# Attention with a cached K and V on one core: K transposed as 64-row tiles into two PSUM banks, P transposed into score banks, loads of 256 KB paced by TensorE operations

## The chip, the cores and the metric

The kernel runs on one core of a Trainium2 chip. The metric is the device time of one execution in microseconds (us). A time below is either the median of unprofiled runs, or comes from one profiled execution, whose trace gives the start and length of every instruction. The engines are TensorE (PE in the profile; PEld is its weight load), VectorE (DVE), ScalarE (ACT), GpSimd (POOL) and SyncE (SP), which issues the loads.

## The reference

Two blocks, A and B, do the same thing with their own data; their outputs are joined on the last axis. All data are bf16. For one block:

```python
B, Sq, D, H, Sk, Dh = 16, 64, 640, 32, 512, 128
q = (x @ wq).reshape(B, Sq, H, Dh).transpose(0, 2, 1, 3)
scores = einsum("bhqd,bhkd->bhqk", q, k_cache) * Dh ** -0.5
p = softmax(scores, axis=-1)
o = einsum("bhqk,bhkd->bhqd", p, v_cache)
out = o.transpose(0, 2, 1, 3).reshape(B, Sq, H * Dh) @ wo
```

K and V of one block are 67 MB each, so 268 MB of cache are read for the two, and with the weights (21 MB) and x about 292 MB. The scores contract over Dh, which is the last axis of K in memory: K has to be transposed on the chip before the score matmul can use it, and P has to be transposed before it meets V.

## The kernel before, in words

**Steps, macros, chunks, groups, passes.** A step is one head of a pair of batches; its 2 x 64 query rows fill 128 partitions. A macro (index m) is two heads, a chunk is two macros (four heads), a group is 16 heads of one pair of batches (four chunks), and a pass is the eight pairs of batches with one half of the heads of one block. There are 4 passes, 32 groups, 128 chunks, 256 macros and 512 steps. One chunk reads 1.05 MB of K and as much of V.

**The work of a macro.** On TensorE: KX transposes K (L451-459), eight 128x128 transposes for each of the two batches (j = 0, 1) into PSUM bank 7; QP2 makes q of two heads (L469, ten matmuls); SM makes the scores of one step (L487, one matmul of 512 columns for each batch, side by side in the two 64-column halves of the array); TR2 transposes P (L528, eight 128x128 transposes into bank 6); PV2 multiplies by V (L549, sixteen matmuls of 64 columns); OP2 multiplies by the first 512 columns of wo (L569, two matmuls). OX does the last 128 columns of wo for a whole group at once (L580, sixteen matmuls), and for the very last group in two parts. The other engines move the results on: KE copies transposed K out of PSUM (DVE, L462, 1024 columns each); QE2 copies q and OE2 copies o (ACT, L482 and L564, 256 columns each); MX takes the row maximum (DVE, L502); EX is the exponential with the row sum (ACT, L508); RC2 the reciprocal (DVE); NM scales P (POOL, L520); TE2 or TA2 copies transposed P out, on DVE (L539) or on ACT (L544). OVP and OXP keep the sum of the first half of the heads in SBUF, OVF and OXF add the second half, ST stores it.

**K by DMA.** In the 11 groups named in TGROUPS (by_dma, L98) the K of the second batch is not transposed by TensorE: one DMA_TRANSPOSE for the whole group (LDKT, L647) writes it to kd_sb, and KX and KE of j = 1 are left out.

**PSUM.** Bank 0 holds the output sum, bank 1 q and o (half each), banks 2 to 5 the scores of four steps in turn, bank 6 transposed P, bank 7 transposed K.

**Order.** Each engine runs a fixed list. The templates PE_T, ACT_T, DVE_T and POOL_T in Cfg (L29-43) give the order of one chunk: a kind, an offset in macros, and a planned time within PERIOD (6.7 us). build_plan (L69) unrolls them. With the offset, KX runs two to four macros ahead of SM of the same macro, PV2 two or three behind it, OP2 three or four behind it. Who waits for whom follows from named resources (the banks, the ring slots, the loaded tiles), and prune_waits (L321) drops waits that others imply. TensorE takes its list strictly in order.

**Loads.** All loads go out from SP, in the order of their planned first use, each as soon as its ring slot is free by the plan (L252-264): K and V in pieces of 512 KB into a K ring of 4 chunks (NKB) and a V ring of 5 (NVB), wq and wo in pieces of 640 KB (four heads) into 6 slots each, x by DMA_TRANSPOSE (LDX, L641). A load waits only for TensorE operations that still read its slot. SP issues in order, so a load that waits holds all later ones.

The lines that the profile names: L457 KX, L466 KE, L475 QP2, L484 QE2, L496 SM, L505 MX, L511 EX, L517 RC2, L525 NM, L534 TR2, L541 TE2, L546 TA2, L558 PV2, L566 OE2, L574 OP2, L584 OX, L602 OVF, L607 OXF, L630 LDWQ, L638 LDWO, L644 LDX, L651 LDKT, L660 LDV, L664 LDK. The functions that the change touches, and what calls them:

Of the kernel before, what the change touches and what calls it, by code (L numbers as in the profile page):

```python
# [14 lines left out]
class Cfg:  # L15
    G = 4
    HH = 16
    NKB = 4
    NW = 6
    TGROUPS = (4, 6, 11, 13, 15, 19, 21, 23, 27, 29, 31)  # L20
    TLEAD = 1.0
    NVB = 5
    XLEAD = 1.5
    NQ = 3
    NKT = 5
    NP = 4
    NPN = 4
    NT = 2
    NO = 9  # L29
    NR = 8  # L30
    NS = 4
    PERIOD = 6.7
    PE_T = (("SM", 0, 0, 0.0), ("SM", 0, 1, 0.21), ("SM", 1, 0, 0.43), ("SM", 1, 1, 0.64), ("KX", 2, 1, 0.98),
            ("PV2", -3, 0, 1.43), ("TR2", -2, 0, 1.9), ("OP2", -4, 0, 2.35), ("KX", 3, 1, 2.78), ("QP2", 3, 0, 3.23),
            ("OP2", -3, 0, 3.79), ("OX", -3, 0, 4.2), ("KX", 3, 0, 4.22), ("PV2", -2, 0, 4.67), ("TR2", -1, 0, 5.14),
            ("KX", 4, 0, 5.59), ("QP2", 4, 0, 6.04))
    ACT_T = (("EX", 0, 0, 1.13), ("OE2", -3, 0, 2.1), ("EX", 0, 1, 2.49), ("TA2", -2, 0, 3.15), ("QE2", 3, 0, 4.0),
             ("EX", 1, 0, 4.4), ("OXP", -3, 0, 5.2), ("OE2", -2, 0, 5.34), ("EX", 1, 1, 5.73), ("OVP", -3, 0, 6.4),
             ("QE2", 4, 0, 6.65), ("ST", -3, 0, 6.68))
    DVE_T = (("MX", 0, 0, 0.44), ("MX", 0, 1, 1.06), ("RC2", -1, 0, 1.66), ("KE", 2, 1, 1.68), ("MX", 1, 0, 2.3),  # L40
             ("TE2", -2, 0, 2.6), ("RC2", 0, 0, 3.3), ("KE", 3, 1, 3.43), ("MX", 1, 1, 4.1), ("KE", 3, 0, 4.87),
             ("OXF", -3, 0, 5.3), ("OVF", -3, 0, 5.5), ("TE2", -1, 0, 5.79), ("KE", 4, 0, 6.4))
    POOL_T = (("NM", -1, 0, 1.95), ("NM", -1, 1, 2.8), ("NM", 0, 0, 4.2), ("NM", 0, 1, 5.05))
    TAIL_SPLIT = 2
    SLOT_NS = 3400.0
    DMA_NS = dict(LDK=3100.0, LDKT=9600.0, LDV=3100.0, LDWQ=3900.0, LDWO=4300.0, LDX=700.0)


class Op:
# [3 lines left out]
    def __init__(self, eng, kind, idx, reads=(), writes=(), dur=0.0, ts=None, aux=None):  # L53
        self.eng = eng
        self.kind = kind
        self.idx = idx
        self.reads = tuple(reads)
        self.writes = tuple(writes)
        self.sem = None
        self.count = None  # L60
        self.deps = []
        self.waits = []
        self.dur = dur
        self.ts = ts
        self.aux = aux
        self.dma = kind in ("LDK", "LDKT", "LDV", "LDX", "LDWQ", "LDWO", "ST")


def build_plan(dims, cfg):  # L69
# [3 lines left out]
    assert H % HH == 0 and HH % G == 0 and G % 2 == 0 and cfg.NR % 2 == 0 and B % 2 == 0  # L73
# [11 lines left out]
    MPP = NBP * MPG  # L85
    MPC = G // 2
# [11 lines left out]
    def by_dma(m, j=1):  # L98
        return j == 1 and m // MPG in cfg.TGROUPS

    tstart = [m for m in range(0, NMAC, MPG) if by_dma(m)]

# [3 lines left out]
    def kslot(m, j):  # L106
        return (4 * (m // 2) + (j if m % 2 == 0 else 3 - j)) % cfg.NKT

    def on_act(m):
        return m % 2 == 0 and not by_dma(min(m + 4, NMAC - 1))  # L110

    def make_op(kind, m, sub, ts):
        g0, g1 = 2 * m, 2 * m + 1
        if kind in ("KX", "KE") and by_dma(m, sub):
            return None
        ps_, bp, grp, h0 = step_info(g0)
        c = g0 // G
        if kind == "KX":
            return mk("pe", "KX", (m, sub), [("kn", c % cfg.NKB, g0 % G), ("kn", c % cfg.NKB, g1 % G), ("ident",)],
                      [("KTB",)], ts)  # L120
        if kind == "KE":
            return mk("dve", "KE", (m, sub), [], [("KTB",), ("ktp", kslot(m, sub))], ts)
        if kind in ("MX", "EX", "NM"):
            g = 2 * m + sub
            r = g % cfg.NR
            if kind == "MX":
                return mk("dve", "MX", g, [], [("SB", g % cfg.NS), ("negmax", r)], ts)
            if kind == "EX":
                return mk("act", "EX", g, [("negmax", r)], [("SB", g % cfg.NS), ("p", g % cfg.NP), ("rowsum", r)], ts)
            return mk("pool", "NM", g, [("p", g % cfg.NP), ("recip", r)], [("pn", g % cfg.NPN)], ts)  # L130
        r0, r1 = g0 % cfg.NR, g1 % cfg.NR
        if kind == "QP2":
            return mk("pe", "QP2", m, [("xT", bp), ("wq", wslot(ps_, h0 // G))], [("QOB",)], ts)
        if kind == "QE2":
            return mk("act", "QE2", m, [], [("QOB",), ("qT", m % cfg.NQ)], ts)
        if kind == "SM":
            kt = [("ktp", kslot(m, 0)), ("kd",) if by_dma(m) else ("ktp", kslot(m, 1))]
            return mk("pe", "SM", (m, sub), [("qT", m % cfg.NQ)] + kt, [("SB", (2 * m + sub) % cfg.NS)], ts)
        if kind == "RC2":
            return mk("dve", "RC2", m, [("rowsum", r0), ("rowsum", r1)], [("recip", r0), ("recip", r1)], ts)  # L140
        if kind == "TR2":
            return mk("pe", "TR2", m, [("pn", g0 % cfg.NPN), ("pn", g1 % cfg.NPN), ("ident",)], [("PTB",)], ts)
        if kind in ("TE2", "TA2"):
            if (kind == "TA2") != on_act(m):
                return None
            return mk("dve" if kind == "TE2" else "act", kind, m, [], [("PTB",), ("pT", m % cfg.NT)], ts)
        if kind == "PV2":
            return mk("pe", "PV2", m, [("pT", m % cfg.NT), ("v", c % cfg.NVB, g0 % G), ("v", c % cfg.NVB, g1 % G)],
                      [("QOB",)], ts)
        if kind == "OE2":  # L150
            return mk("act", "OE2", m, [], [("QOB",), ("oT", m % cfg.NO)], ts)
        if kind == "OP2":
            return mk("pe", "OP2", m, [("oT", m % cfg.NO), ("wo", wslot(ps_, h0 // G))], [("OUTB",)], ts)
        lo = grp * MPG
        last = h0 + 2 == SPB
        if kind == "OX":
            hi = m + 1
            if grp == NGRP - 1 and h0 + 6 == SPB:
                pass
            elif not last:  # L160
                return None
            elif grp == NGRP - 1:
                lo = m - 1
            return mk("pe", "OX", m, [("oT", i % cfg.NO) for i in range(lo, hi)]
                      + [("wo", wslot(ps_, i)) for i in sorted({(2 * i % SPB) // G for i in range(lo, hi)})],
                      [("SB", 0)], ts, aux=(lo, hi))
        if not last:
            return None
        if kind in ("OVP", "OXP") and ps_ % NHALF == 0:
            return mk("act", kind, m, [], [("OUTB",) if kind == "OVP" else ("SB", 0), ("outp", bp, kind[1])], ts,  # L170
                      aux=grp)
        if kind in ("OVF", "OXF") and ps_ % NHALF == 1:
            return mk("dve", kind, m, [("outp", bp, kind[1])],
                      [("OUTB",) if kind == "OVF" else ("SB", 0), ("out_sb", kind[1])], ts, aux=grp)
        if kind == "ST" and ps_ % NHALF == 1:
            return mk("act", "ST", m, [("out_sb", "V"), ("out_sb", "X")], [("out_dram", grp)], ts, aux=grp)
        return None

    templates = {"pe": cfg.PE_T, "dve": cfg.DVE_T, "pool": cfg.POOL_T, "act": cfg.ACT_T}
    at = {}  # L180
    for eng, tmpl in templates.items():
        offs = [t[1] for t in tmpl]
        for k in range(-(max(offs) + 1) // 2 - 1, (NMAC - min(offs)) // 2 + 1):
            for kind, off, sub, t in tmpl:
                m = 2 * k + off
                if 0 <= m < NMAC:
                    op = make_op(kind, m, sub, 2 * k + 2 * t / cfg.PERIOD)
                    if op is not None:
                        progs[eng].append(op)
                        at[kind, m, sub] = op.ts  # L190
# [10 lines left out]
    for ps_ in range(NPASS):  # L201
        for j in range(HG):
            m0 = ps_ * MPP + j * MPC
            i = ps_ * HG + j
            rq = ro = NEG
            if i >= cfg.NW:
                end = ((i - cfg.NW) // HG + 1) * MPP
                rq = at["QP2", end - MPG + ((i - cfg.NW) % HG) * MPC + MPC - 1, 0]
                ro = at["OX", end - 1, 0]
            add(rq, at["QP2", m0, 0], at["QP2", m0, 0], 0, "LDWQ", (ps_, j), [("wq", wslot(ps_, j))], (ps_, j),  # L210
                cfg.DMA_NS["LDWQ"] * G / 8.0)
            add(ro, at["OP2", m0, 0], at["OP2", m0, 0], 3, "LDWO", (ps_, j), [("wo", wslot(ps_, j))], (ps_, j),
                cfg.DMA_NS["LDWO"] * G / 8.0)

    def tload(m):
        return at["SM", m, 0] - cfg.TLEAD

# [540 lines left out]
```

## Time and profile before

| what | value |
|---|---|
| median of 3 runs | 898.71 us (897.31 to 901.26) |
| the profiled execution's own time | 900.23 us |
| its span, first to last instruction | 898.5 us |
| instructions | 33204 |
| mean granted TensorE clock | 0.996 |
| loaded and stored by DMA | 296.81 MB, mean 330 GB/s |
| issues of K and V | 211 of K and 254 of V with 512 KB, 2 and 4 with 256 KB |
| K by DMA_TRANSPOSE | 11 issues, median 17.9 us to landing |

Busy times are summed lengths of instructions. A matmul's length in the trace is its latency, and neighbours overlap, so what a block of matmuls costs is read from the distance between the start of its first and the start of the next block's first. The same holds for VectorE and ScalarE, where the end of one instruction overlaps the start of the next.

### The profile page before, as it was taken

How to read it: one execution, taken by the hardware profiler on the slowest of the kernel's cores; microseconds unless marked ns; L12 is line 12 of the kernel's file. 1: busy time of each engine (PE TensorE's matmuls, PEld its weight loads, DVE VectorE, ACT ScalarE, POOL GpSimd, SP SyncE). 2: the span in 40 equal slices, each digit the busy share in tenths (PEclk: the TensorE clock that was granted, in tenths of full speed). 3: DMA queues.
4: the chain of work that ended last, by engine and by line, in shares of the span. 5: the costliest groups of instructions: out<-in, count | busy, mean ns of one | idle time of the engine just before them, and what ended most of it. 6: DMA issues, size and time to landing. Idle time of an engine off the chain costs nothing.

```text
span 898.5 us, 33204 instructions
## 1 busy us (share of the span) xinstructions
PE 857.5 (95%) x14016; PEld 691.1 (77%) x14144; DVE 746.6 (83%) x1398; ACT 628.0 (70%) x1651; POOL 413.8 (46%) x518
## 2 busy tenths in 40 slices
PE   4999989999999999999998998999999999999997
PEld 3777777878888877878786787778778777787875
DVE  2888878888888888888887887888888798888896
ACT  1776766777777777767676776777777676776774
POOL 0544444445444454544444444445454444545453
PEclk9999999999999999999999999999999999999999
DMA  9999999999999999999999999999999999999992
GB/s 304 336 340 365 318 272 365 295 361 365 363 366 368 286 361 322 319 369 270 364 361 368 367 260 365 309 324 366 294 363 363 367 370 284 367 286 365 315 333 77
DMA packets 315172, 296.81 MB, mean 330 GB/s; under 512 B 109200, under 2 KB 260752, under 8 KB 315024
## 3 DMA queue, kind: packets, MB, share of 16 engines
q1 hardware_dynamic: 312720, 292.06, 106.3%
q10 hardware_dynamic: 2304, 2.62, 0.9%
q8 instruction: 111, 1.82, 0.9%
q14 instruction: 37, 0.30, 0.1%
HBM read 266.34 MB, written 2.62 MB: 299 GB/s over the span
## 4 chain that ended last, share of the span: by engine, by line
PE 78%; DMA 9%; SPq 7%; DVE 3%; issue 1%; ACT 1%; DVEq 0%; ACTq 0%
PE ps L457 20%; PE ps L475 14%; PE ps L496 12%; PE ps L558 11%; PE ps L534 10%; PE ps L574 9%; DMA kn_ring<-in_B_k_cache_dram 5%; DMA kn_ring<-in_A_k_cache_dram 4%; SPq L651 3%; PE ps L584 3%; SPq L644 2%; DVE ktp_ring L466 1%; SPq L664 1%; DMA wq_sb<-in_A_wq_dram 1%; DVE negmax L505 1%
## 5 line engine op out<-in xcount | busy, mean ns | idle before, releaser
L525 POOL TENSOR_SCALAR pn_ring<-p_ring,recip 128x512 bf16<-128x512 bf16 x512 | 413.1, 843 | 476.1 <-DVE recip L517 475.7
L511 ACT ACTIVATE p_ring<-ps,negmax 128x512 bf16<-128x512 f32 x512 | 350.1, 684 | 100.0 <-DVE negmax L505 100.0
L466 DVE COPY ktp_ring<-ps 128x1024 bf16<-128x1024 bf16 x424 | 290.0, 684 | 82.1 <-PE ps L457 67.2
L505 DVE TENSOR_REDUCE negmax<-ps 128x1 f32<-128x512 f32 x512 | 337.3, 680 | 15.2 <-PE ps L496 4.9
L457 PEld LDWEIGHTS ps<-ident,kn_ring 128*128 128x128 bf16 x3392 | 205.3, 98 | 108.5 <-issue 46.5
L457 PE MATMUL ps<-ident,kn_ring 128*128 128x128 bf16 x3392 | 263.6, 221 | 21.1 <-DMA kn_ring<-in_A_k_cache_dram 11.8
L475 PE MATMUL ps<-xT_sb,wq_sb 128*128 128x128 bf16 x2560 | 187.8, 221 | 1.3 <-DMA wq_sb<-in_A_wq_dram 0.6
L558 PE MATMUL ps<-pT_ring,v_ring 128*128 128x64 bf16 x4096 | 162.0, 193 | 8.6 <-DMA v_ring<-in_B_v_cache_dram 3.1
L475 PEld LDWEIGHTS ps<-xT_sb,wq_sb 128*128 128x128 bf16 x2560 | 154.4, 99 | 16.9 <-ACT oT_ring L566 15.8
L558 PEld LDWEIGHTS ps<-pT_ring,v_ring 128*128 128x128 bf16 x4096 | 141.9, 98 | 28.5 <-issue 26.5
L484 ACT ACTIVATE qT_ring<-ps 128x256 bf16<-128x256 f32 x256 | 98.3, 384 | 86.1 <-PE ps L475 86.0
L534 PE MATMUL ps<-ident,pn_ring 128*128 128x128 bf16 x2048 | 156.4, 219 | 0.0
L566 ACT ACTIVATE oT_ring<-ps 128x256 bf16<-128x256 f32 x256 | 97.6, 381 | 75.3 <-PE ps L558 68.1
L541 DVE COPY pT_ring<-ps 128x1024 bf16<-128x1024 bf16 x174 | 119.5, 687 | 35.5 <-PE ps L534 35.5
L496 PE MATMUL ps<-ktp_ring,qT_ring 128*64 128x512 bf16 x848 | 137.3, 391 | 0.0
L574 PE MATMUL ps<-wo_sb,oT_ring 128*128 128x512 bf16 x384 | 124.5, 379 | 6.8
L534 PEld LDWEIGHTS ps<-ident,pn_ring 128*128 128x128 bf16 x2048 | 118.5, 98 | 0.0
L511 ACT ACTIVATION_READ_ACCUMULATOR p_ring<-ps,negmax 128x1 f32 x512 | 103.1, 201 | 0.0
L546 ACT ACTIVATE pT_ring<-ps 128x1024 bf16<-128x1024 bf16 x82 | 84.0, 1024 | 0.0
L496 PEld LDWEIGHTS ps<-ktp_ring,qT_ring 128*64 128x64 bf16 x848 | 47.1, 110 | 41.0 <-issue 2.1
L517 DVE RECIPROCAL recip<-rowsum 128x2 f32<-128x2 f32 x256 | 40.9, 160 | 14.7 <-ACT p_ring L511 14.6
L496 PE MATMUL ps<-kd_sb,qT_ring 128*64 128x512 bf16 x176 | 47.0, 390 | 0.0
(15 smaller groups left out, 152.0 us busy)
## 6 DMA issues: line engine op xcount, KB each, us to landing
v_ring<-in_A_v_cache_dram SPq DMA_DIRECT2D x128, 512.0 KB, 9.9
v_ring<-in_B_v_cache_dram SPq DMA_DIRECT2D x126, 512.0 KB, 9.8
kn_ring<-in_A_k_cache_dram SPq DMA_DIRECT2D x108, 512.0 KB, 9.4
kn_ring<-in_B_k_cache_dram SPq DMA_DIRECT2D x103, 512.0 KB, 9.3
wq_sb<-in_A_wq_dram SPq DMA_DIRECT2D x8, 640.0 KB, 9.9
wo_sb<-in_A_wo_dram SPq DMA_DIRECT2D x8, 640.0 KB, 10.7
wq_sb<-in_B_wq_dram SPq DMA_DIRECT2D x8, 640.0 KB, 9.7
wo_sb<-in_B_wo_dram SPq DMA_DIRECT2D x8, 640.0 KB, 10.3
```

What stands on the lines that cost most here:

```text
L457: ins = e.transpose(kt_ps[:, t8, :], kn_ring[:, c % NKB, j, hp, t8, :], ident[:, :])
L466: ins = e.tensor_copy(dst, src)
L475: ins = e.matmul(q_ps[:, sub * 128:(sub + 1) * 128], wq_sb[:, wslot(ps_, hh // G), kt, (hh % G) * DH:(hh % G + 1) * DH], xT_sb[:, kt, bp * ...
L484: ins = e.activation(qT_ring[:, m % NQ].rearrange("p s q -> p (s q)"), q_ps, ACTF.Copy, scale=scale)
L496: ins = e.matmul(s_bank(2 * m + sub)[64 * j:64 * j + 64, :], qT_ring[:, m % NQ, sub, 64 * j:64 * j + 64], kt, start=True, stop=True, tile_ ...
L505: ins = e.reduce_max(negmax[:, r:r + 1], s_bank(g), axis=AX.X, negate=True)
L511: ins = e.activation(p_ring[:, g % NP, :], s_bank(g), ACTF.Exp, bias=negmax[:, r:r + 1], scale=1.0, accum_out=rowsum[:, r:r + 1])
L525: ins = e.tensor_scalar(dst, src, recip[:, r:r + 1], 1.0, ALU.mult, ALU.mult)
L534: ins = e.transpose(pt_ps[:, sub, t, :], pn_ring[:, g % NPN, t * 128:(t + 1) * 128], ident[:, :])
L541: ins = e.tensor_copy(pT_ring[:, m % NT].rearrange("p s t q -> p (s t q)"), pt_ps_flat)
L558: ins = e.matmul(o_ps[:, col:col + 64], v_ring[:, c % NVB, j, gi, t, :], pT_ring[:, m % NT, sub, t, 64 * j:64 * j + 64], start=(t == 0), s ...
L574: ins = e.matmul(out_ps, oT_ring[:, m % NO, sub, :], wo_sb[:, wslot(ps_, hh // G), hh % G, 0:N0], start=(hh == 0), stop=(hh == SPB - 1))
```

## The change

- KX becomes one operation for a macro: 32 transposes of 64 rows by 128 columns in place of two times eight of 128 by 128. The two 64-row halves of a K tile (they are the two heads) are row tiles of the array, named in turn, and each half writes its own bank, 6 or 7. KE copies both banks in one instruction of 2048 columns.
- There is no K by DMA: kd_sb, LDKT and TGROUPS go, and the 88 KX and KE of those groups come back.
- TR (P of a macro, eight 128x128 transposes as before) writes into score bank 2 or 3 once the scores there are used up. Bank 6 becomes free for K. TE alternates: even macros on DVE, odd ones on ACT.
- q and o go by chunks: QP4, QE4, PV4 and OE4 do four heads, in the whole of bank 1, taken in turn by q and o. OX writes to bank 4 in place of bank 2, and always the whole group at once.
- Rings: K in 10 units of a macro (NKU) in place of 4 chunks, transposed K in 3 macros, qT 4, pT 4, oT 10 macros.
- Loads: K, V in pieces of 256 KB (one batch and two heads), wq and wo in pieces of 320 KB.
- pace_loads replays the TensorE list with a duration per operation (PE_NS), a cost for each change of tile mode (MODE_NS) and a rate for each kind of load. Where the load queue of that replay would hold more than QUEUE_NS of work, the load gets a wait on the TensorE operation that ends just before its turn.

The core of the diff:

```diff
-    NKB = 4
+    NKU = 10
...
-    TGROUPS = (4, 6, 11, 13, 15, 19, 21, 23, 27, 29, 31)
...
-    PERIOD = 6.7
...
+    PERIOD = 6.15
+    PE_T = (("SM", 0, 0, 0.0), ("SM", 0, 1, 0.21), ("SM", 1, 0, 0.43), ("SM", 1, 1, 0.64), ("KX", 2, 0, 0.96),
+            ("PV4", -2, 0, 1.53), ("OP", -5, 0, 2.47), ("TR", -2, 0, 2.9), ("KX", 3, 0, 3.45), ("TR", -1, 0, 4.03),
+            ("OP", -4, 0, 4.47), ("OX", -5, 0, 4.9), ("QP4", 2, 0, 4.92))
+    ACT_T = (("EX", 0, 0, 1.13), ("EX", 0, 1, 1.79), ("OVP", -5, 0, 2.92), ("OE4", -2, 0, 2.95), ("EX", 1, 0, 3.52), ("EX", 1, 1, 4.18),
+             ("TE", -1, 0, 4.84), ("OXP", -5, 0, 5.9), ("ST", -5, 0, 6.0), ("QE4", 2, 0, 6.27))
+    DVE_T = (("MX", 0, 0, 0.44), ("MX", 0, 1, 1.06), ("KE", 2, 0, 1.68), ("RC2", 0, 0, 2.83), ("OVF", -5, 0, 2.92),
+             ("MX", 1, 0, 2.97), ("MX", 1, 1, 3.59), ("TE", -2, 0, 4.21), ("KE", 3, 0, 4.83),
+             ("OXF", -5, 0, 5.9), ("RC2", 1, 0, 5.98))
+    POOL_T = (("NM", 0, 0, 3.0), ("NM", 0, 1, 3.85), ("NM", 1, 0, 6.1), ("NM", 1, 1, 6.95))
...
+    PE_NS = dict(SM=213.0, KX=464.0, TR=447.0, PV4=932.0, QP4=1118.0, OP=432.0, OX=893.0)
+    MODE_NS = 108.0
+    QUEUE_NS = 800.0
+    START_NS = 1030.0
+    RATE = dict(LDK=384.0, LDV=344.0, LDWQ=344.0, LDWO=354.0, LDX=160.0)
...
+        if kind == "TR":
+            return mk(eng, "TR", m, [("pn", g0 % cfg.NPN), ("pn", g1 % cfg.NPN), ("ident",)], [("SB", m % 2)], ts)
+        if kind == "TE":
+            return mk(eng, "TE", m, [], [("SB", m % 2), ("pT", m % cfg.NT)], ts)
...
+    t_sp, t_q, n = 0.0, 0.0, 0
+    gates = []
+    for op in sp:
+        advance()
+        ready = max([t_sp] + [ends[id(d)] for d in op.deps if d.eng == "pe"])
+        start = max(t_q, ready + cfg.START_NS)
+        issue = start - cfg.START_NS - cfg.QUEUE_NS
+        while n < len(done) and ends[id(done[n])] <= issue:
+            n += 1
+        gate = done[n - 1] if n and ends[id(done[n - 1])] > ready else None
+        gates.append(gate)
+        if gate is not None:
+            ready = ends[id(gate)]
+        t_q = start + nbytes(op) / cfg.RATE[op.kind]
+        t_sp = ready + 400.0
+        arrive[id(op)] = t_q + 1300.0
+    for op, gate in zip(sp, gates):
+        if gate is not None:
+            op.deps.append(gate)
...
+        OUT_BANK, QO_BANK, S_BANK0, KT_BANK = 0, 1, 2, 6
...
+        kt_ps = [ps[:, KT_BANK + r, :].bitcast(BF16) for r in range(2)]
+        kt_ps_both = ps[:, KT_BANK:KT_BANK + 2, :].bitcast(BF16)
...
         def em_KX(e, op):
-            m, j = op.idx
-            g0 = 2 * m
-            c, hp = g0 // G, (g0 % G) // 2
             first = last = None
-            for t8 in range(8):
-                ins = e.transpose(kt_ps[:, t8, :], kn_ring[:, c % NKB, j, hp, t8, :], ident[:, :])
-                first = first or ins
-                last = ins
+            for j in range(2):
+                for t in range(8):
+                    for r in range(2):
+                        half = slice(64 * r, 64 * r + 64)
+                        ins = e.transpose(kt_ps[r][:, 64 * (8 * j + t):64 * (8 * j + t) + 64],
+                                          kn_ring[half, op.idx % NKU, j, t, :], ident[half, half],
+                                          tile_position=(64 * r, 0))
+                        first = first or ins
+                        last = ins
             return first, last
...
+            ins = e.tensor_copy(ktp_ring[:, op.idx % NKT].rearrange("d r j s -> d r (j s)"), kt_ps_both)
...
-            src = blocks[blk][1][2 * bp + 1, h0:h0 + HH].rearrange("h (p t) d -> (h p) (t d)", t=8)
-            ins = e.dma_start_transpose(kd_sb[:, :, :], src)
...
+            src = blocks[blk][1][2 * bp + j, h0:h0 + 2].rearrange("hs (p t) d -> (hs p) (t d)", t=8)
+            ins = e.dma_start(kn_ring[:, m % NKU, j].rearrange("p t d -> p (t d)"), src)
```

## The prediction, made blind

> **What bounds the kernel now.** First the page: busy time by engine, and the chain that ended last.
>
> ```profile
> PE 857.5 (95%) x14016; PEld 691.1 (77%) x14144; DVE 746.6 (83%) x1398; ACT 628.0 (70%) x1651; POOL 413.8 (46%) x518
> ...
> PE 78%; DMA 9%; SPq 7%; DVE 3%; issue 1%; ACT 1%; DVEq 0%; ACTq 0%
> ```
>
> TensorE carries 78% of the chain; loads and the load queue (DMA, SPq) carry 16%. So there are stretches with two different limits. The windows show them (length, then PE, PEld, DVE, ACT, POOL busy, then clock, DMA share, GB/s):
>
> ```profile
> 120.00:130.00 10.00, 9.31 (x155) 7.39 (x154) 9.00 (x18) 7.89 (x21) 5.88 (x8) 1.00 1.19 240
> 130.00:140.00 10.00, 7.30 (x92) 5.45 (x94) 4.87 (x10) 3.77 (x11) 2.69 (x4) 0.83 1.08 367
> ...
> 200.00:290.00 90.00, 89.31 (x1491) 73.36 (x1503) 78.19 (x145) 68.53 (x176) 42.18 (x52) 1.00 1.08 366
> ...
> 872.00:878.00 6.00, 5.95 (x103) 4.82 (x101) 4.75 (x11) 3.91 (x11) 3.20 (x4) 1.00 1.10 349
> ```
>
> From 200 to 290 us TensorE never waits while 366 GB/s come in. At 120 us the rate drops to 240, and after it TensorE starves (7.30 of 10, clock 0.83). The chain of waits there names the cause: the transposing load of a TGROUPS group holds SP's queue for 13.48 us, and the K piece behind it lands 7.13 us later.
>
> ```profile
> 111.76 13.48 SPq L651
> ...
> 126.46 7.13 DMA kn_ring<-in_A_k_cache_dram
> ```
>
> Now the price of each TensorE block, by distances between starts in the timeline of TensorE, one whole chunk from SM to SM:
>
> ```profile
> 401.81 1.05 PE L496 MATMUL ps<-ktp_ring,qT_ring 128*64 128x512 bf16 x8
> 402.80 0.62 PE L457 MATMUL ps<-ident,kn_ring 128*128 128x128 bf16 x8
> 403.26 0.63 PE L558 MATMUL ps<-pT_ring,v_ring 128*128 128x64 bf16 x16
> 403.73 0.61 PE L534 MATMUL ps<-ident,pn_ring 128*128 128x128 bf16 x8
> 404.39 0.38 PE L574 MATMUL ps<-wo_sb,oT_ring 128*128 128x512 bf16 x1
> 404.60 0.61 PE L457 MATMUL ps<-ident,kn_ring 128*128 128x128 bf16 x8
> 405.05 0.72 PE L475 MATMUL ps<-xT_sb,wq_sb 128*128 128x128 bf16 x10
> 405.61 0.59 PE L574 MATMUL ps<-wo_sb,oT_ring 128*128 128x512 bf16 x2
> 406.04 0.61 PE L457 MATMUL ps<-ident,kn_ring 128*128 128x128 bf16 x8
> 406.49 0.63 PE L558 MATMUL ps<-pT_ring,v_ring 128*128 128x64 bf16 x16
> 406.95 0.61 PE L534 MATMUL ps<-ident,pn_ring 128*128 128x128 bf16 x8
> 407.44 0.62 PE L457 MATMUL ps<-ident,kn_ring 128*128 128x128 bf16 x8
> 407.89 0.72 PE L475 MATMUL ps<-xT_sb,wq_sb 128*128 128x128 bf16 x10
> 408.54 1.05 PE L496 MATMUL ps<-ktp_ring,qT_ring 128*64 128x512 bf16 x8
> ```
>
> KX costs 0.45, PV2 0.465, TR2 0.465 (mean of 0.49 and 0.87 less an OP2), QP2 0.56, OP2 0.43, so 0.215 per matmul of 512 columns. SM is four pairs, 0.86 at that price, but takes 0.99: leaving the column-tile mode costs 0.13. QP2 ahead of SM takes 0.65: entering costs 0.09. So one mode change is about 0.11. The chunk is 6.73; OX (412.77 to 413.66, 0.89 a group) adds 0.22: 6.95. A TGROUPS chunk lacks two KX: 6.04. With 11 of 32 groups the mean is 6.64. The span follows: first SM at 18.90, 127 chunks of 6.64 = 843, last SM (883.63) to the end 14.9: 877. The span is 898.5, so about **22 us are stalls**, mostly after transposing loads, in the first 70 us, and where new weights come in (480 to 560 us).
>
> **The change, part by part.**
>
> *KX.* Per macro 16 transposes of 128 columns go, 32 of 64 columns come. No row shows 64-row tiles. A floor: a matmul of 64 columns costs 0.029 (PV2, 0.465 / 16), two row tiles at best run at once, so 16 x 0.029 = 0.464. An upper end: no overlap, 32 x 0.029 = 0.928. For overlap speaks the score matmul, whose two tiles start together and cost 0.21 to 0.22 a pair, the price of one:
>
> ```profile
> 872.06 0.38 PE L496 MATMUL ps<-ktp_ring,qT_ring 128*64 128x512 bf16 x1
> 872.06 0.38 PE L496 MATMUL ps<-kd_sb,qT_ring 128*64 128x512 bf16 x1
> ```
>
> Those are column tiles with 512 columns behind each weight load; a 64-column transpose has a load of its own, so the row does not prove it. I take 0.464, the pair as the nearest row. The Trainium skill ("TensorEngine Tiling (Array Packing)", section Key Properties) says that tiles run weight loads and matmuls in parallel; by it too the sum is the one below, and by the PV2 row alone it would be the first rival.
>
> *Mode changes.* KX becomes a mode of its own: SM to KX, KX to PV4, TR to KX, KX to TR, QP4 to SM, five a chunk where there were two. The three new ones: bounded by 0 and by twice the dearer row (0.26); I take 0.11.
>
> *The new chunk on TensorE:* SM 0.86, KX 0.93, PV 0.93, TR 0.93, QP 1.12, OP 0.86, five changes 0.55, OX 0.22: **6.40**. Against 6.64 that is 0.24 x 127 = 30 us less. Against a plain chunk it is 0.55 less; the groups that had K by DMA become 0.36 dearer.
>
> *Other engines, by chunk.* DVE: four MX at 0.61 (spacing of neighbours), two KE, one TE 0.61, two RC2 at 0.1, OVF and OXF 0.1. A KE of 1024 costs 0.59; one of 2048 lies between that and 1.18; taken 1.18. Sum 5.7. ACT: four EX at 0.66, TE 0.94, QE4 and OE4 at 0.60 (the 128x512 OVP row, 596 ns; they were 0.38 for half), OVP and OXP 0.1: 4.9. POOL 4 x 0.84. All lie beside TensorE's 6.40. If DVE's cover went, KX is late next, since both K banks are reused at once: KE must end before the next KX, and the planned times leave 0.6 to 1.1.
>
> *Banks.* TR into score banks costs nothing while TE is done before the same bank's next SM: planned TE on ACT ends at 4.84 + 0.94 = 5.78, that SM comes at 6.15 + 0.21 = 6.36. One q/o bank makes PV4 wait for QE4 and QP4 for OE4, with 0.8 and 1.4 of planned room.
>
> *Loads.* The eleven transposes go, and with them the stalls behind them; same bytes, at the rate of the plain window: 292 MB / 366 = 798 us, 6.18 a chunk (2.26 MB). TensorE wants 6.40, so the loads keep up by 3% only; in a pass, once the weights are in, K and V alone want 2.10 / 0.366 = 5.7 and the rings fill. At the start they do not: by SM of chunk 4, K of six chunks, V of three, 5.2 MB of weights and 0.7 MB of x make 15 MB or 42 us, plus the first issue (2.2) and slow x transposes (some 3), 47, against 18.9 + 25.6 = 44.5 on TensorE. I keep 5 us of stalls (3 to 8) of the 22.
>
> *SP.* 1094 issues in place of about 515. One of 512 KB takes 0.49 to 0.58 in an empty queue; one of half size at most that: 635 us in all, beside 850. The new waits stand in SP's list: behind one wait all later loads, and behind those KX first, then PV4. The replay sets them only where more than 0.8 us of loads are queued, so a wait should find the queue still filled. Taken as nothing; the second rival is the case where it isn't.
>
> *Ends.* Before the first SM the old list needs K of two chunks, the new one of one; some 3 us earlier, which the loads of the next chunks take back. The tail stays near 15: OX is no longer split, PV comes by chunks, but KX and QP are out of the way. Bounds minus 3 and plus 4; taken at 0.
>
> **Sum.** 18.9 + 127 x 6.40 + 5 + 15 = 852, which is 47 below the span. The profiled execution took 900.2, its span plus 1.7; the median is 898.7. From the median: 898.7 - 47 = 852. **I predict 852.** The pieces' spread (mode changes by a third, stalls 3 to 8, tail) gives 838 to 868. A difference of 0.5% (4.5 us) is about what a measurement of this kernel can tell from no change.
>
> **Rivals.**
>
> *1. Row tiles do not overlap; slower.* Place: inside KX. Each transpose brings its own weight load, and the fastest rate of load and matmul in the trace is 0.029 a pair (PV2). Then KX is 0.928, a chunk 7.33, the sum 852 + 0.464 x 254 = 970. It decides from a KX of 0.464 + 47 / 254 = 0.65 upward. Against it: the score pair. 0.14.
>
> *2. The loads set the end.* If the paced pieces of 256 KB do not keep the queue full, the rate falls. The only row with such pieces, at 872 to 878, ran at 349, though those were mostly V with short packets. 292 / 349 = 837, plus 2 at the start and 18 from the last landing (about 880) to the end: 857. At the old mean of 330 GB/s it is 905. Taken 857 to 885. 0.13. The Trainium skill ("DMA: Bandwidth & Descriptors", Rules for kernel authors) speaks against the change here: it wants 1 MiB or more in a DMA for full bandwidth. The trace got 366 GB/s from 512 KB with a full queue; no run so far shows 256 KB throughout.
>
> *3. Mode changes or a bank cost more.* At 0.22 for each new change, or with ScalarE's TE 0.3 late for the next SM in each chunk, it is about 40 more: 868 to 893. The planned room of 0.58 speaks against the latter. 0.10.
>
> *4. Less than that:* changes into and out of row tiles cost nothing; then 6.07, below the loads' 6.18, and the loads end it at 798 + 20 = 818 to 838. 0.05.
>
> **How the numbers follow.** The forecast, 838 to 868, has 0.58. The range of 8 in 10 goes from 834 to 893: it takes in rival 3, most of 2 and the edge of 4, and leaves out rival 1. Faster by over 0.5%: the forecast, rival 4, nearly all of 2 and 3, together 0.82. Slower: rival 1 and the far end of 2, 0.15. Between: 0.03.
>
> **What would show it.** Right: distance from KX to the next block about 0.57 (0.464 and a change), SM to SM 6.2 without OX, GB/s at 350 to 366 with no dips, no SPq in the chain. Rival 1: the distance near 1.0. Rival 2: waits of KX on kn_ring and a DMA share below 1. Rival 3: PE idle ahead of SM with ACT's pT_ring as releaser, or KX to PV4 over 0.7. The prediction is wrong if KX costs over 0.65 or the mean rate stays below 340.

## The result, and the profile after

The changed kernel takes 907.5 us (median of 17 runs, 900.9 to 922.05) where the kernel before takes 900.0 (17 runs, 897.0 to 904.6). The ratio is 1.0069, 95% interval 1.0048 to 1.0089; ratios, here and below, leave out the runs that took over 1.5% more than the fastest of the same kernel (here 915.4 and 922.0 us), and are not the quotients of the medians. So the change makes the kernel slightly slower; 852 was predicted. The profiled execution took 908.6 with a span of 906.8.

From the page of the changed kernel: busy time by engine, mean rate, the queue that carries TensorE's instructions, the chain of waits by engine, and one landing row (issue to landing, median us).

```profile
PE 836.8 (92%) x18944; PEld 643.6 (71%) x18944; DVE 722.4 (80%) x1184; ACT 652.5 (72%) x1441; POOL 416.8 (46%) x518
...
DMA packets 245373, 297.51 MB, mean 328 GB/s; under 512 B 28096, under 2 KB 179648, under 8 KB 245184
...
q8 instruction: 151, 2.47, 1.1%
...
PE 80%; DMA 12%; issue 3%; DVE 3%; ACT 1%; SPq 1%; DVEq 0%; ACTq 0%
...
v_ring<-in_A_v_cache_dram SPq DMA_DIRECT2D x256, 256.0 KB, 5.4
```

The load queue has left the chain (SPq 7% before, 1% now), as the change meant it to. But DMA grew from 9% to 12%, "issue" from 1% to 3%, and the rate is no higher than before (328 GB/s against 330). "issue" is time in which TensorE waited for nothing that the profile shows. Queue q8 has 151 packets; on the page of the kernel before it had 111:

```profile
q8 instruction: 111, 1.82, 0.9%
```

TensorE's list itself became as short as planned. One undisturbed chunk in the timeline of TensorE (start, us):

```profile
402.79 1.05 PE L497 MATMUL ps<-ktp_ring,qT_ring 128*64 128x512 bf16 x8
403.77 0.64 PE L465 MATMUL ps<-ident,kn_ring 64*128 64x64 bf16 x32
404.35 1.11 PE L556 MATMUL ps<-pT_ring,v_ring 128*128 128x64 bf16 x32
...
406.26 0.64 PE L465 MATMUL ps<-ident,kn_ring 64*128 64x64 bf16 x32
406.84 0.62 PE L535 MATMUL ps<-ident,pn_ring 128*128 128x128 bf16 x8
...
408.94 1.05 PE L497 MATMUL ps<-ktp_ring,qT_ring 128*64 128x512 bf16 x8
```

KX with its change of mode is 404.35 - 403.77 = 0.58, and SM to SM is 6.15 (0.57 and 6.18 were predicted). So the loss is in stalls. Taken by distances from SM to SM: the 127 distances sum to 875.1 us. Of these 127 x 6.15 = 781 are the chunk, 35 are OX, and **59 are stalls**; the same sum for the kernel before (864.7 us, of which 844 are its list, redone with the measured chunks) has 21. The stalls are of two kinds. The chain of waits shows the first, at 283 us: SP holds a load of V back until a TensorE operation has ended (at 282.89), issues it, and PV4 waits for its landing.

```profile
282.91 1.34 SPq L660
284.25 0.04 issue
284.30 4.58 DMA v_ring<-in_A_v_cache_dram
288.87 0.14 issue
289.01 1.09 PE ps L556 x32
```

The second kind has no releaser. Timeline of TensorE of the same kernel (the brackets give the idle time ahead and what ended it):

```profile
251.12 0.45 PE L535 MATMUL ps<-ident,pn_ring 128*128 128x128 bf16 x5
252.37 0.33 PE L535 MATMUL ps<-ident,pn_ring 128*128 128x128 bf16 x3 [0.79 <-issue]
```

Eight transposes of one operation, with nothing to wait for between them, are cut in two. Counting TensorE's instructions from the start of the list, with the weight loads and the few that only wait, such cuts fall at the same place: 191 to 195 in a block of 256. The instructions come in packets of 16,384 bytes on q8, and 38,723 instructions in 151 packets are 256 to a packet, 64 bytes each. The cuts come once in each packet's worth of instructions, so the reading is that TensorE **waits for its own instructions**; e1 below shows the packets landing just before TensorE goes on. (Why the place is 191 to 195 and not 256 the trace does not show; the count starts with the first instruction that it has.) The Trainium skill ("Runtime: NRT & Kernel Launch", section Instruction fetch mechanics) states the refill in blocks of 16 KiB, 256 instructions, and says that crossing one is "mostly hidden". The trace agrees on the block and not on the hiding, and the measurement decides.

For every kernel below, **late time** is worked out from the trace thus: the distance from one TensorE weight load to the one before, less the median of that distance at the same place in the list, summed where it is over 0.06 us. What falls at 191 to 195 of a block is put down to the fetch. The rest, counted after the first 30 us, is mostly data, and with it up to some 10 us in which the list itself varies (OX has two lengths) or another engine is waited for. Each sum comes from the one profiled execution of its kernel, which lay up to 9 us from the median (e1 at 939.7, e5 at 1026.5).

### The profile page after: what moved, and what is told of

Its sections match the earlier page's. It is cut to its first block, busy times and chain, and to the rows that moved or that the text cites. A ratio compares the mean times of both kernels' runs of the same rounds, so it can differ in the third digit from the quotient of the medians.

```text
span 906.8 us, 43761 instructions
## 1 busy us (share of the span) xinstructions
PE 836.8 (92%) x18944; PEld 643.6 (71%) x18944; DVE 722.4 (80%) x1184; ACT 652.5 (72%) x1441; POOL 416.8 (46%) x518
## 4 chain that ended last, share of the span: by engine, by line
PE 80%; DMA 12%; issue 3%; DVE 3%; ACT 1%; SPq 1%; DVEq 0%; ACTq 0%
PE ps L481 14%; PE ps L465 14%; PE ps L556 14%; PE ps L497 12%; PE ps L535 12%; PE ps L572 11%; DMA v_ring<-in_A_v_cache_dram 5%; PE ps L582 3%; DMA kn_ring<-in_B_k_cache_dram 3%; DMA v_ring<-in_B_v_cache_dram 2%; DVE negmax L506 1%; DMA wq_sb<-in_A_wq_dram 1%; ACT p_ring L512 1%; DMA kn_ring<-in_A_k_cache_dram 1%; DVE out_sb L600 1%
## 5 line engine op out<-in xcount | busy, mean ns | idle before, releaser
L473 DVE COPY ktp_ring<-ps 128x2048 bf16<-128x2048 bf16 x256 | 312.5, 1221 | 24.3 <-PE ps L465 24.0
L465 PEld LDWEIGHTS ps<-ident,kn_ring 64*128 64x128 bf16 x8192 | 136.2, 95 | 85.9 <-issue 67.9
L465 PE MATMUL ps<-ident,kn_ring 64*128 64x64 bf16 x8192 | 168.0, 191 | 17.7 <-issue 9.5
L481 PE MATMUL ps<-xT_sb,wq_sb 128*128 128x128 bf16 x2560 | 168.1, 221 | 13.6 <-DMA wq_sb<-in_A_wq_dram 10.2
L572 PE MATMUL ps<-wo_sb,oT_ring 128*128 128x512 bf16 x512 | 153.8, 382 | 3.0 <-issue 1.5
L544 ACT ACTIVATE pT_ring<-ps 128x1024 bf16<-128x1024 bf16 x128 | 131.1, 1024 | 12.4 <-PE ps L535 11.8
L490 ACT ACTIVATE qT_ring<-ps 128x512 bf16<-128x512 f32 x128 | 76.5, 597 | 73.1 <-PE ps L481 73.1
L546 DVE COPY pT_ring<-ps 128x1024 bf16<-128x1024 bf16 x128 | 87.4, 683 | 17.1 <-PE ps L535 17.0
L564 ACT ACTIVATE oT_ring<-ps 128x512 bf16<-128x512 f32 x128 | 76.3, 596 | 26.7 <-PE ps L556 24.9
L582 PEld LDWEIGHTS ps<-wo_sb,oT_ring 128*128 128x128 bf16 x512 | 29.4, 98 | 16.7 <-ACT p_ring L512 13.9
```

What stands on the lines that cost most here:

```text
L465: ins = e.transpose(kt_ps[r][:, 64 * (8 * j + t):64 * (8 * j + t) + 64], kn_ring[half, op.idx % NKU, j, t, :], ident[half, half], tile_pos ...
L473: ins = e.tensor_copy(ktp_ring[:, op.idx % NKT].rearrange("d r j s -> d r (j s)"), kt_ps_both)
L481: ins = e.matmul(qo_ps[:, i * 128:(i + 1) * 128], wq_sb[:, wslot(ps_, hh // G), kt, i * DH:(i + 1) * DH], xT_sb[:, kt, bp * 128:(bp + 1) * ...
L544: ins = e.activation(dst, pt_bank(op.idx), ACTF.Copy)
L546: ins = e.tensor_copy(dst, pt_bank(op.idx))
L572: ins = e.matmul(out_ps, oT_ring[:, m % NO, sub, :], wo_sb[:, wslot(ps_, hh // G), hh % G, 0:N0], start=(hh == 0), stop=(hh == SPB - 1))
```

## The experiments

The first theory (A in the expectations) was that the waits of pace_loads make the loads late: its replay ends at 832 us, gives 922 of the 1094 loads a wait, and counts on as little as 3.8 us from the release of a load to its landing, where the trace has 5.4 from issue to landing. Its rivals stand in the expectations. The results together, with the packets on q8 in brackets, ratios to the kernel before, and late time in us:

| kernel | TensorE instructions | median us | ratio (95%) | late at 191-195 | late elsewhere |
|---|---|---|---|---|---|
| before | 28,615 (111) | 900.0 | 1 | 1 | 31 |
| after | 38,723 (151) | 907.5 | 1.0069 (1.0048-1.0089) | 34 | 33 |
| e1 no waits | 38,723 | 948.0 | 1.0556 (1.0517-1.0595) | 90 | 11 |
| e2 4 us queued | 38,723 | 887.5 | 0.9874 (0.9839-0.9909) | 39 | 14 |
| e3 no waits, 512 KB | 38,723 | 954.9 | 1.0602 (1.0568-1.0636) | 103 | 11 |
| e4 waits, 512 KB | 38,723 | 915.7 | 1.0172 (1.0134-1.0210) | 41 | 31 |
| e5 before, more instructions | 40,903 (159) | 1017.2 | 1.1330 (1.1268-1.1392) | 128 | 5 |
| e6 no waits, full tiles | 30,531 (119) | 918.3 | 1.0213 (1.0178-1.0249) | 1 | 11 |
| e7 5 loads at once | 38,723 | 1019.4 | 1.1344 (1.1297-1.1390) | 2 | 82 |
| e8 8 loads at once | 38,723 | 901.4 | 0.9975 (0.9936-1.0014) | 44 | 12 |
| f4 7 loads at once | 38,723 | 887.8 | 0.9872 (0.9833-0.9910) | 20 | 29 |
| f1 half full tiles, no waits | 34,627 (135) | 912.2 | 1.0149 (1.0107-1.0191) | 32 | 12 |
| f2 half full tiles, 4 us | 34,627 | 890.8 | 0.9909 (0.9875-0.9942) | 14 | 12 |
| f3 quarter full tiles, 4 us | 36,675 (143) | 891.4 | 0.9913 (0.9882-0.9944) | 25 | 12 |
| g1 after, V not reloaded | 38,477 (150) | 861.6 | 0.9592 (0.9572-0.9611) | 12 | 2 |
| g2 before, V not reloaded | 28,536 (111) | 881.0 | 0.9806 (0.9785-0.9828) | 0 | 16 |

### Taking the waits away

```diff
+    GATES = False
...
-        if gate is not None:
+        if gate is not None and cfg.GATES:
```

> The changed kernel without the waits that pace_loads adds (922 of the 1094 loads carry one); pieces, rings and all engine lists as in the change. Theory A, the added waits: they hold loads back until a fixed TensorE operation, the loads take 5.4 us to land where the replay counts on about 3.8, so TensorE waits a little in many chunks (66 us in all above 127 chunks of 6.15 and the OX). Without them the loads run ahead as far as the rings allow, the rate goes to 360 or more while data is wanted, and the time falls to 845 to 865. Theory B, the pieces of 256 KB are slow by themselves: the rate stays near 345 and the time near 890 to 907. Theory C, TensorE order or the smaller rings cause the waits: near 907 too, with waits on other engines.

Measured: 948, slower than with the waits. Theory A falls as it stood. Yet one half of it came true: late time for data went from 33 to 11. What came in its place is the other kind. In the timeline of TensorE of this kernel the 20 matmuls of one QP4 are cut in two:

```profile
286.20 0.67 PE L482 MATMUL ps<-xT_sb,wq_sb 128*128 128x128 bf16 x9
288.86 1.02 PE L482 MATMUL ps<-xT_sb,wq_sb 128*128 128x128 bf16 x11 [2.00 <-issue]
```

and the chain of waits of its page has 10% "issue":

```profile
PE 81%; issue 10%; DVE 3%; SPq 3%; DMA 2%; ACT 2%; POOL 0%; DVEq 0%; ACTq 0%
```

Of its 64 gaps of over 0.9 us between two weight loads after 20 us, 47 stand at 192 to 195 of a block, and each of these ends 1.2 to 1.6 us after a q8 packet has come in. The packets themselves take about as long in every kernel (medians 0.99 to 1.10 us), so they are not slow: they start late.

### More in the queue, and larger pieces

e2 sets `QUEUE_NS = 4000.0`, so that loads may go out earlier. e3 is e1 with K and V in pieces of 512 KB, e4 the changed kernel with such pieces and its waits:

```diff
-            src = blocks[blk][1][2 * bp + j, h0:h0 + 2].rearrange("hs (p t) d -> (hs p) (t d)", t=8)
+            src = blocks[blk][1][2 * bp:2 * bp + 2, h0:h0 + 2].rearrange("b hs (p t) d -> (hs p) b (t d)", t=8)
```

> The changed kernel with the waits kept, but with 4.0 us of queued loads allowed in the replay in place of 0.8 (QUEUE_NS). Theory A: the same loads are released 3.2 us earlier, which is more than the 1.6 us by which they land late, so most of the 66 us of stalls go: 850 to 875. Theory B: no change, 890 to 907.

> No added waits, and K and V in pieces of 512 KB (both batches of a macro; four heads of a batch). Theory A: size matters little, within 1% of the run without waits and 256 KB. Theory B: faster than that run by the difference between 345 and 366 GB/s, some 5%.

> The added waits kept at 0.8 us of queue, pieces of 512 KB. Theory A: as slow as the change or slower, 900 to 920, since a larger piece behind a late wait lands later. Theory B: 855 to 875.

Measured: 887 (faster than both kernels, though not in the range that A gave), 955 and 916 (both as expected). With 3.2 us more in the replay's queue, late time for data falls from 33 to 14, while that of the fetch does not fall (34 and 39). And 256 KB is not the trouble: without waits 512 KB is no faster (955 against 948), and with them it is slower (916 against 907.5). The Trainium skill ("DMA: Bandwidth & Descriptors", Rules for kernel authors) wants 1 MiB or more per DMA for full bandwidth; doubling the piece brought nothing here, with several out at once. No run here loads K or V in pieces of 1 MiB.

### Is it the number of instructions?

Theory F: packets of instructions come late behind queued loads, which shows when a block of 256 is used up faster than the next arrives. e5 gives the kernel *before* more instructions for the same columns: q in matmuls of 64 columns in place of 128, wo in eight of 64 in place of one of 512 (each is its own sum, so the sum over heads in the first 512 output columns is left out). e6 is e1 with KX in full 128x128 tiles: half the instructions of KX, for about twice its time.

```diff
+                for w in range(8):
+                    ins = e.matmul(out_ps[:, 64 * w:64 * w + 64], oT_ring[:, m % NO, sub, :],
+                                   wo_sb[:, wslot(ps_, hh // G), hh % G, 64 * w:64 * w + 64], start=True, stop=True)
...
+                    ins = e.transpose(kt_ps[j][:, 128 * t:128 * t + 128], kn_ring[:, op.idx % NKU, j, t, :], ident[:, :])
```

> The kernel before with 12,300 more TensorE instructions for the same work per column: QP2 in two matmuls of 64 columns in place of one of 128, OP2 in eight of 64 in place of one of 512 (each head then overwrites its part of the output sum, so the sum over heads in the first 512 output columns is left out). Loads as before, unpaced. Theory F, the instruction fetch: TensorE's instructions come in blocks of 256 (16 KB) over the same DMA engines, and behind a deep queue of loads a block comes late; a block now lasts 256 / 318 x 6.8 = 5.5 us where it lasted 7.6. Then gaps at instruction 193 of a block appear, which the kernel before does not have, and the time rises by 50 to 90 us: 950 to 990. Rival: TensorE pays only for the narrower matmuls, 0.1 a chunk: 905 to 920, with no such gaps.

> The changed kernel without the added waits and with KX as 16 transposes of 128x128 a macro in place of 32 of 64 rows (each batch into its own bank; KE reorders). 64 instructions fewer a chunk of 296. Theory F: a chunk costs 6.7 and 0.22 for OX, a block lasts 7.4 us, the 90 us of gaps at instruction 193 that the unpaced change shows go away nearly all: 127 x 6.95 + 34 + 10 to 20 = 925 to 940, less than the unpaced change (948) though each chunk is 0.55 dearer. Rival, the unpaced loads hurt TensorE in another way (memory ports, late waits): the stalls stay, 127 x 6.95 + 34 + 100 = about 1015.

Measured: 1017 and 918. e5 lies above F's range, e6 below it; both on F's side. More instructions, with no change in array tiles, pieces or waits, cost the kernel before 117 us. The sum nearly closes: 128 us of late time appear at 191 to 195, 26 us of it elsewhere go away (31 to 5), and the narrower matmuls themselves cost some 15 (a plain chunk takes 6.85 where it took 6.73), which makes 117, where the profiled executions differ by 126. In e5's timeline of TensorE an OP2 is cut:

```profile
404.82 0.34 PE L577 MATMUL ps<-wo_sb,oT_ring 128*128 128x64 bf16 x6
406.12 0.45 PE L577 MATMUL ps<-wo_sb,oT_ring 128*128 128x64 bf16 x10 [0.97 <-issue]
```

e6 has the deeper queue of e1 and no such gap. Its chunk has 64 TensorE instructions fewer and is 0.54 us longer, so a packet lasts 7.4 us in place of 5.4. By itself e6 would leave open that the row tiles cause the gaps; e5, which has none, rules that out as the only cause. The stretch from 300 to 350 us shows it at one rate (length, then PE, PEld, DVE, ACT, POOL busy, clock, DMA share, GB/s); first e1, then e6:

```profile
300.00:350.00 50.00, 43.27 (x984) 33.57 (x992) 38.73 (x64) 34.51 (x76) 21.58 (x27) 1.00 1.07 368
```

```profile
300.00:350.00 50.00, 49.41 (x823) 40.80 (x829) 41.67 (x68) 35.90 (x80) 23.16 (x29) 1.00 1.08 370
```

The loads run equally full in both; TensorE waits 6.7 us in one and 0.6 in the other.

### Is it the queue's depth?

pace_loads gives way to a plain rule: a load waits for the landing of the load W places before it in SP's list (so at most W are out).

```diff
-    pace_loads(progs, cfg, nbytes)
+    for i, op in enumerate(progs["sp"]):
+        if i >= cfg.WINDOW:
+            op.deps.append(progs["sp"][i - cfg.WINDOW])
```

> The changed kernel with the pacing replaced: a load waits until the fifth load before it has landed, so at most 5 x 256 KB are queued, and never fewer while the rings have room. Theory F: the queue is short (3.6 us at 360 GB/s), so blocks of instructions come nearly in time (gaps at instruction 193 under 20 us in all), and loads may run ahead of TensorE, so data stalls stay under 25 us: 850 to 880. Rival, the data rate needs a deeper queue: under 345 GB/s, over 890.

> As the window of 5, with 8 loads outstanding (2 MB, 5.7 us). Theory F: more gaps at instruction 193 (30 to 50 us) and fewer data stalls (under 15): 870 to 895, slower than the window of 5. Rival: faster than the window of 5.

> The changed kernel with a window of seven loads in place of the added waits. Five loads gave 293 GB/s with 4.4 us to landing, eight 333 with 5.7; seven outstanding are 1.8 MB. Theory F: data stalls 12 to 20, gaps at instruction 193 near 30: 809 + 34 + 45 = 885 to 895.

Measured: 1019, 901 and 888. At five the kernel becomes bound by its loads: the expected 850 to 880 was wrong and the rival right, since five do not reach the rate. So e8 is not slower than e7, and it lies above its 870 to 895 too (ten runs, 889.5 to 906.5). f4 met its range, but with its parts the other way round: 29 us for data and 20 for the fetch, where 12 to 20 and 30 were expected.

With five out the fetch is hardly ever late (2 us, with 38,723 instructions), but this alone does not isolate the depth, since TensorE's other waits stretch a packet there (1015 / 151 = 6.7 us with them). e1 and e8 do: the same list, as little late time elsewhere (11 and 12), a mean rate that is no lower (333 GB/s in e8, 317 in e1), and with eight out in place of no limit 44 us of fetch in place of 90. f4 goes the same way (20), though part of that may lie hidden behind its longer waits for data. So the depth is the other half of F.

The traces give the delay itself. With packets and blocks counted alike from the start, no packet of the kernels with this list starts before TensorE is at about instruction 170 of the packet's own block, and where TensorE stands, it stands at 191 to 195 of the next block: a packet has about one block's time to start and to land. From instruction 192 of its block to the start of the packet the median is 0.8 us in g1 (below), 1.7 with five loads out, 2.5 with seven, 2.9 with eight and 3.3 with no limit. With 1.1 for the packet and 1.4 from its landing until TensorE goes on, that makes 3.3, 4.2, 5.0, 5.4 and 5.8, where a block lasts 5.4 us; the kernel before has 3.2, so 5.7, where its block lasts 7.6. Around these medians the packets scatter by some 1 to 3 us, so the late time grows by degrees.

From the page of e7:

```profile
DMA packets 245376, 297.53 MB, mean 293 GB/s; under 512 B 28096, under 2 KB 179648, under 8 KB 245184
...
DMA 91%; PE 4%; SPq 3%; issue 1%; DVE 1%; ACT 0%; DVEq 0%; ACTq 0%
...
kn_ring<-in_A_k_cache_dram SPq DMA_DIRECT2D x256, 256.0 KB, 4.4
```

Five pieces of 262 KB (1.31 MB) in 4.4 us are 298 GB/s: what is out, divided by the landing time, is the rate. With seven it is 336 GB/s in the mean at 5.2 to 5.3, with eight 333 at 5.7 to 5.8: an eighth piece adds landing time and no rate. The late times go over from data to fetch: 82 and 2 at five, 29 and 20 at seven, 12 and 44 at eight.

### A mixture

f1 is e1 with KX of every second macro in full tiles, f2 the same with waits for a queue of 4 us, f3 with every fourth.

```diff
+            if op.idx % 2 == 1:
+                for j in range(2):
+                    for t in range(8):
+                        ins = e.transpose(kt_ps[j][:, 128 * t:128 * t + 128], kn_ring[:, op.idx % NKU, j, t, :], ident[:, :])
```

> The changed kernel without the added waits; KX of odd macros as 16 full tiles, of even macros as 32 row tiles. 264 TensorE instructions a chunk, a chunk between 6.15 and 6.69 (taken 6.42, and 0.22 for OX): a block of 256 instructions lasts 6.4 us. Theory F: the gaps at instruction 193 are set by the block's duration against the time a fetch takes behind a deep queue (about 6 us: 0.6 us late a block at 5.3, none at 7.4), so some 0 to 15 us remain of 90: 127 x 6.64 + 34 + 10 + 0 to 15 = 887 to 902. Rival, row tiles as such cause the gaps: half of them stay, 45 us: 930.

> The same mix of tiles, with the added waits at 4 us of queue. Theory F: gaps at instruction 193 under 5 us, data stalls 13 as in the run with 4 us: 843 + 34 + 13 + 5 = 890 to 900; a little slower than row tiles throughout at 4 us (887), since the cheaper fetch no longer pays the dearer chunk.

> One KX in four as full tiles, added waits at 4 us of queue. 280 instructions a chunk of 6.5: a block lasts 5.9 us. Theory F: gaps at instruction 193 half of the 39 us: 827 + 34 + 13 + 20 = 885 to 897, within 1% of row tiles throughout (887).

Measured: 912, 891, 891. f1 missed: at 135 packets 32 us of fetch remained where 0 to 15 were expected, so there is no sharp point but a slope. How long a block lasts is 256 x chunk time / instructions in a chunk. Unpaced, late fetch a block is 0.6 us where it lasts 5.4 us (e1, 90 us in 151), 0.24 at 6.4 (f1, 32 in 135) and 0.01 at 7.4 (e6, 1 in 119). f2 and f3 hit their times, though with more fetch left than expected (14 where under 5, 25 where 20 were). What they win in fetch (39 to 14 and 25) goes into the longer transposes (0.54 us for each chunk with both in full tiles, so 0.27 and 0.14, or 34 and 17 us over 127 chunks): neither beats e2.

### The list without the loads' pressure

g1 is e1, and g2 the kernel before, with V loaded only into the first filling of its ring; later chunks read what lies there, so the reload of V is left out of the computation. The edit of g1 (that of g2 skips the same loads):

```diff
-            for i in (2 * j, 2 * j + 1):
+            for i in (2 * j, 2 * j + 1) if c < cfg.NVB else ():
```

> The changed kernel without the added waits, and V is loaded for the first five chunks only; later chunks multiply by the V that stands in the ring, so nearly half of the bytes are left out and all TensorE instructions stay. Theory F: with the DMA engines half idle the blocks of instructions come in time, gaps at instruction 193 under 5 us, no data stalls after the start: 15 + 127 x 6.37 + 16 = 840 to 848, which is what the new TensorE list would cost with its feeds in time. Rival, the row tiles make TensorE wait by themselves: most of the 90 us stays, 900 or more.

> The kernel before with V loaded for the first five chunks only, in the same way. It loses only its 22 us of data stalls: 872 to 882. The distance between the two runs is then what the new TensorE list is worth: 30 to 35 us.

Measured: 861.6 and 881.0; g2 as expected, g1 above its 840 to 848. In g1's page the chain of waits is TensorE's alone:

```profile
PE 90%; DVE 3%; SPq 2%; ACT 2%; issue 2%; DMA 1%; POOL 0%; DVEq 0%; ACTq 0%
```

With 38,477 instructions and 196 GB/s in the mean, the fetch is late only in the first 96 us (12 us in all; after that there is one wait of 0.3), while the rings are still being filled. Two windows of g1 show the rate fall and TensorE's waits end (in the order of the windows above):

```profile
60.00:80.00 20.00, 19.09 (x440) 14.62 (x438) 15.52 (x26) 14.44 (x34) 8.12 (x11) 1.00 1.07 359
100.00:120.00 20.00, 20.00 (x478) 15.47 (x476) 18.06 (x31) 16.10 (x37) 9.87 (x13) 1.00 0.53 173
```

After that nearly every chunk of g1 takes 6.15, or with OX 7.06 or 7.54. The 19.4 us between g2 and g1 (30 to 35 were expected), and those 12, are about 30: what the new list is worth when it is fed. The miss is the 12 us and OX.

## Why the prediction was wrong, point by point

**The list was priced right.** KX at 0.464 with a mode change of 0.11 (0.57; measured 0.58), chunk 6.18 without OX (6.15), stalls before 22 (21). So row tiles overlap, and rival 1 (970) is out. Without stalls the changed kernel would be 15.4 to the first SM, 781 and 35 of chunks and 16.3 of tail: 848, where the prediction without its 5 us of stalls had 847.

**One term was mis-sized: OX.** 0.22 a chunk was taken, 0.28 came (35.4 / 127, some 7 us). In passes that end a sum, OX takes 1.39 in place of 0.91, because it waits for its score bank. In g1, with its data there, the timeline of TensorE shows OX starting 0.91 us after an OP that costs 0.43:

```profile
403.94 0.59 PE L573 MATMUL ps<-wo_sb,oT_ring 128*128 128x512 bf16 x2
404.85 1.07 PE L583 MATMUL ps<-wo_sb,oT_ring 128*128 128x128 bf16 x16 [0.32 <-ACT p_ring L513]
```

A shorter chunk and nearer ends gave nearly all of those 7 us back (4 and 2).

**The steps that failed are *Loads* and *SP*.** *Loads*: "I keep 5 us of stalls (3 to 8) of the 22." It was 59. *SP*: "so a wait should find the queue still filled. Taken as nothing." It did not, and e2 shows it: with more queued, 20 us are gone (907.5 to 887.5), and what went is late data (33 to 14). This is rival 2's mechanism, which had 0.13; by itself it would have given 848 + 25 = 873, within its 857 to 885. That its 905 at 330 GB/s lies near the measured time is luck: a mean rate is the bytes over the span, whatever made the span long.

**The other half was in no rival: *KX* put the instructions at nothing.** About 34 of the 59 us are TensorE waiting for instructions; the other 25 are data. The step counted "32 of 64 columns" as time and never as instructions: 64 with their weight loads in place of 32, for half the time. With the K that DMA had transposed, the list went from 28,615 to 38,723, so that a packet lasts 5.4 us rather than 7.6. The window that carried the load sum, 366 GB/s with TensorE never waiting, was true of a list with 7.6 us to a packet. e1 has 368 GB/s from 300 to 350 us and TensorE busy for 43.3 of 50; e5 and e6 show that the count does it, e1 beside e8 and g1 that the queue's depth does.

**So the two halves pull against each other.** Loads early enough for the data (e1: 11 us late) cost 90 us of fetch; a queue short enough for the fetch (e7: 2 us) costs 82 of data. The waits of pace_loads, which looked like the fault, take 56 us off the fetch. The sum of the prediction, 852, would need both ends at once, and with this number of instructions no version here had them: the best are e2 and f4, both 1.3% faster than the kernel before.

Of the signs that were named, "the mean rate stays below 340" came true (328). "no SPq in the chain", a sign of being right, all but came true as well (1%) while the time was missed: a chain without SPq does not tell whether a load was issued in time.

**What stays open.** Why a packet starts late behind a deep queue: that it does is measured, but the trace has no request for it, so that it takes its turn behind loads in the same DMA engines is argued from e1, e8 and g1 and not shown. Not tried: the same row tiles with fewer instructions elsewhere, as q for two pairs of batches in matmuls of 256 columns, which by e6 and f1 may be where more lies.

## What to carry to other kernels

Count instructions as well as columns: a change that does the same streaming in more instructions moves the time at which the engine needs its next packet, and here this cost time only while many loads were queued. An engine's gap without a releaser, inside a run of like instructions, is to be looked at by its place modulo 256 in the engine's list. Where loads are held back by a rule, take the landing time that the rule counts on from the trace under load, and try its depth in both directions, since here both sides were dear.

## What the runs showed of the hardware

- TensorE's instructions come in packets of 16,384 bytes on q8, which take 1.0 to 1.1 us each and start later the more loads are queued (0.8 to 3.3 us after instruction 192 of a block, in g1, e7, f4, e8 and e1). With eight loads of 256 KB out, or no limit, 5.4 us to a packet was too short (44 and 90 us late in all); 7.4 us (e6, 256 KB) and 7.6 us (before, 512 KB) were enough with no limit (1 us).
- Five loads of 256 KB out at once gave 293 GB/s at 4.4 to 4.5 us to landing, seven 336 at 5.2 to 5.3; eight gave no more (333 at 5.7 to 5.8).
- Two 64-row transposes on two row tiles cost 0.029 us the pair (in the trace of the changed kernel the two start 3 to 4 ns apart and the next pair 25 to 26 ns later), the price of one matmul of 64 columns (PV4, 32 in 0.94). A KX of 32 takes 0.58 to the next block, so about 0.11 are the change of mode.
